# Chunked attention and a squared-ReLU FFN on one core: weight preparation moved from GpSimd to VectorE, the second token tile transposed by TensorE, fewer loads for v

## The chip, the core and the metric

The kernel runs on one core of a Trainium2 chip. The metric is the device time of one execution in microseconds. The engines are named as in the profile: PE (TensorE, the matrix engine; PEld is its weight load), DVE (VectorE), ACT (ScalarE), POOL (GpSimd) and SP (SyncE, which issues all DMAs here). Each engine works off its own instructions strictly in order and waits for others by semaphores.

## The reference: what is computed

Attention inside chunks of 64 tokens, without any link between chunks, followed by a two-layer FFN over all tokens. Shapes: 8 batches, 8 heads, 576 tokens, head dimension 64; the FFN goes 512 -> 2048 -> 512 over 4608 tokens.

```python
scores = scale * np.matmul(q_c, k_c.transpose(0, 1, 2, 4, 3))      # 64x64 per chunk
scores = scores - np.max(scores, axis=-1, keepdims=True)
attn = np.exp(scores)
attn = attn / (np.sum(attn, axis=-1, keepdims=True) + 1e-09)
out = np.matmul(attn, v_c)
x = out.transpose(0, 2, 1, 3).reshape(B * S, H * D)
h = x @ w_in
g = np.where(h >= 1, h, np.where(h <= -1, 0.0, (h + 1) ** 2 / 4))
return (g @ w_out).astype(np.float32)
```

q, k and v are float32; the two weight matrices arrive as float64, 8 bytes an element.

## The kernel before, in words

**Tiles.** The 4608 tokens are nine tiles of 512: tiles 0 to 3 and 5 to 8 are the first 512 tokens of a batch each, tile 4 (`BATCH[4]` is None) collects the last 64 tokens of all eight. In each tile, attention runs in four groups `g` of two heads; the FFN runs in 16 steps `j`, one per block of 128 hidden units.

**Precision.** FFN products use the fast fp32r type with operands split in a high and a low part: `high x high + high x low + low x high`, three matmuls of 512 columns each. `ffn_in` (L528) does twelve per step, `ffn_out` (L563) twelve, two steps behind. `ffn_split` (L548, L549) splits the activation, `attn_split` (L512, L513) the attention output.

**Weight preparation.** There are 32 weight blocks, 16 of `w_in` (wi) and 16 of `w_out` (wo). `load_weight` brings one as raw 64-bit words, 512 KB, into a tile that its two parts later overwrite. `prepare` turns the words into fp32 and splits them. Its steps, in order: ACT copies the upper words' absolute value (L257); DVE raises it to a least value (L260); DVE shifts and masks (L262); DVE merges sign and exponent bits in (L266); ACT scales the lower words to their share of the mantissa (L270); POOL adds the two as integers (L275); ACT rounds to the high part (L282); DVE subtracts for the low part (L286). All preparation happens beside the FFN of the first tile; from then on the weights stay on the chip.

**Attention.** `load_heads` loads q, k and v of a group. `attn_turn` transposes q and k, `scores_of` multiplies, `attn_softmax` normalises (in the first two tiles the last multiply, L477, is on POOL), then the exponentials `e` are transposed to `aT`, `values_of` multiplies by v, and `attn_split` hands on. There are two ways to transpose. In tile 0, PE does it: `flip` (L358) is four 128 x 128 transposes into a PSUM bank, and ACT copies the bank out (L373, L496). From tile 1 on, q and k are loaded block by block (`load_blocks`, L317, four DMAs each) so that a DVE transpose of 32 x 32 blocks finishes the job (L367); `e` is transposed by DVE too (L499) and put in place by eight small DMAs on SP (L489). v is loaded by four DMAs per group (L336).

**What sets the order.** Nothing is reordered by a compiler. `Plan` collects every piece of work with an engine, an estimated cost and what it reads and writes; `Plan.emit` then runs a small list scheduler over these estimates and issues the instructions of each engine in the order in which they would start. `lag` and `moving` are estimates for a DMA's delay and transfer; `port=True` marks pieces that the scheduler keeps from overlapping between DVE and POOL. While PE has nothing to do at the start it is given filler matmuls (L673) until a named PSUM bank is first written. The attention of tile t+1 is planned into the FFN of tile t, one group per four steps; for tile 0, all four groups come first: turn, scores and softmax of each, then values of each. `first_loads` lists the loads of the start in order, with all of v at the end, in front of the first wo block.

Of the kernel before, what the change touches and what calls it, by code (L numbers as in the profile page):

```python
# [9 lines left out]
F32 = mybir.dt.float32  # L10
# [121 lines left out]
def kernel(  # L132
# [15 lines left out]
    nc = tc.nc  # L148
# [46 lines left out]

    o_pair, a_pair = bank_pair("ps_o23"), bank_pair("ps_a")
    o_banks = buffers(psum, "ps_o", 2) + [(f"ps_o{2 + b}", o_pair[:, b, :]) for b in range(2)]
    h_banks = buffers(psum, "ps_h", 2)


# [31 lines left out]
    def load_weight(w, j):  # L232
        def emit():
            words[w, j] = dst = place("words", w, j, [P, 2 * T], U32)
            if w == "wi":
                nc.sync.dma_start(
                    out=dst.rearrange("p (kc f) -> p kc f", kc=KC),
                    in_=w_in[:, 2 * j * P:2 * (j + 1) * P].rearrange(
                        "(kc p) f -> p kc f", p=P
                    ),  # L240
                )
            else:
                nc.sync.dma_start(out=dst, in_=w_out[j * P:(j + 1) * P, :])

        plan.add("sp", 0.6, emit, (), (f"{w}{j}_0", f"{w}{j}_1"), lag=1.7, moving=1.7)

    def prepare(w, j):


        both = (f"{w}{j}_0", f"{w}{j}_1")  # L250
        ykey, yf = turn_of("tmp", tmp_bufs)
        y = yf.bitcast(U32)

        def half(n):
            return words[w, j].rearrange("p (n two) -> p n two", two=2)[:, :, n]

        plan.add("act", 0.52, lambda: nc.scalar.activation(  # L257
            out=yf, in_=half(1).bitcast(F32), func=AF.Abs
        ), both, (ykey,))
        plan.add("dve", 0.34, lambda: nc.vector.tensor_scalar_max(yf, yf, LEAST), (), (ykey,),  # L260
                 port=True)
        plan.add("dve", 0.34, lambda: nc.vector.tensor_scalar(  # L262
            out=y, in0=y, scalar1=3, scalar2=0x3FFFFFFF,
            op0=ALU.logical_shift_left, op1=ALU.bitwise_and,
        ), (), (ykey,), port=True)
        plan.add("dve", 0.6, lambda: nc.vector.scalar_tensor_tensor(  # L266
            out=y, in0=half(1), scalar=0xC0000000, in1=y,
            op0=ALU.bitwise_and, op1=ALU.bitwise_or,
        ), both, (ykey,), port=True)
        plan.add("act", 0.52, lambda: nc.scalar.activation(  # L270
            out=half(0), in_=half(0), func=AF.Copy, scale=2.0 ** -29
        ), (), both)

        def round_up():
            nc.gpsimd.tensor_tensor(out=y, in0=y, in1=half(0), op=ALU.add)  # L275
            words.pop((w, j))

        plan.add("pool", 1.25, round_up, (*both, ykey), (ykey,), port=True)

        def high():  # L280
            weight[w, j] = place("parts", w, j, [P, 2, T], F32R)
            nc.scalar.copy(out=weight[w, j][:, 0, :], in_=yf)  # L282

        def low():
            hi, lo = (weight[w, j][:, n, :] for n in range(2))
            nc.vector.tensor_tensor(out=lo, in0=yf, in1=hi.bitcast(F32), op=ALU.subtract)  # L286
# [40 lines left out]

    def load_values(dst, src, t, g):


        for r in range(2):
            for h in range(2):
                rows = heads_rows(src, t, 2 * g + h)
                into = dst[r * C:(r + 1) * C, h * HALF:(h + 1) * HALF]
                split = "(r n) p d -> r p n d" if t == 0 else "(n r) p d -> r p n d"
                nc.sync.dma_start(  # L336
                    out=into.rearrange("p (n d) -> p n d", d=D),
                    in_=rows.rearrange(split, r=2)[r],
                )

    def load_heads(t, g, which="qkv"):
        for n, src, bufs in (("q", q, q_bufs), ("k", k, k_bufs), ("v", v, v_bufs)):
            if n not in which:
                continue
            key, dst = room(n, bufs, t, g)
            load = load_values if n == "v" else load_rows if t == 0 else load_blocks
            rows, parts = (1.4, 2) if load == load_rows else (1.4, 4) if load == load_values else (
                (2.2, 4) if BATCH[t] is not None else (2.2, 8)
            )
            plan.add(  # L350
                "sp", 0.6 * parts, lambda load=load, dst=dst, src=src: load(dst, src, t, g),
                (), (key,), lag=1.7, moving=rows,
            )

    def flip(ps, src):
# [4 lines left out]
    def attn_turn(t, g):  # L360
        for n, (name, bufs, src_bufs, dst_bufs) in enumerate(
            (("q", "qT", q_bufs, qT_bufs), ("k", "kT", k_bufs, kT_bufs))
        ):
            skey, src = room(name, src_bufs, t, g)
            dkey, dst = room(bufs, dst_bufs, t, g)
            if t > 0:
                plan.add("dve", 0.6, lambda src=src, dst=dst: nc.vector.transpose(  # L367
                    out=dst, in_=src
                ), (skey,), (dkey,))
                continue  # L370
            pkey, ps = o_banks[n]
            plan.add("pe", 0.45, lambda src=src, ps=ps: flip(ps, src), (skey,), (pkey,), columns=T)
            plan.add("act", 0.48, lambda ps=ps, dst=dst: nc.scalar.copy(out=dst, in_=ps),  # L373
                     (pkey,), (dkey,))

    def scores_of(t, g):

        qkey, qT = room("qT", qT_bufs, t, g)  # L380
# [2 lines left out]

        def emit():
            for n in range(CT // 2):
                place = (2 * (n % 2) + n // 2 if t == 0 else n) * C
                for i in range(2):
                    for half in range(2):
                        rows = slice(half * C, (half + 1) * C)
                        at = slice((2 * n + i) * C, (2 * n + i + 1) * C)  # L390
                        nc.tensor.matmul(  # L391
                            out=pair[i * C:(i + 1) * C, half, place:place + C],
                            lhsT=qT[rows, at], rhs=kT[rows, at], start=True, stop=True,
                        )

# [2 lines left out]
    def values_of(t, g):  # L398
# [6 lines left out]
        def emit():  # L405
            for n in range(CT // 2):
                for h in range(2):
                    at = (4 * (n % 2) + 2 * (n // 2) + h) * C if t == 0 else h * HALF + n * C
# [25 lines left out]
    def attn_softmax(t, g):  # L434
# [4 lines left out]
        akey, aT = room("aT", aT_bufs, t, g)  # L439
        e3 = e.rearrange("p (n k) -> p n k", k=C)  # L440
        e4 = e.rearrange("p (h n k) -> p h n k", h=2, k=C)
        mx4 = mx.rearrange("p (h n) x -> p h n x", h=2)
        sc = pair[:, :, :HALF].rearrange("p h (n k) -> p h n k", k=C)

        plan.add("dve", 0.6, lambda: nc.vector.tensor_reduce(  # L445
# [3 lines left out]
        if sums:  # L449
            plan.add("dve", 0.08, lambda: nc.vector.tensor_scalar_mul(mx, mx, -SCALE), (), (mkey,))  # L450

            def exps():
                for n in range(G):
                    nc.scalar.activation(
                        out=e3[:, n, :], in_=sc[:, n // 4, n % 4, :], func=AF.Exp, bias=mx[:, n, :],
                        scale=SCALE, accum_out=sm[:, n, :],
                    )

            plan.add("act", 2.33, exps, (*pkeys, mkey), (ekey, skey))
# [18 lines left out]
            out=e3, in0=e3, in1=sm.broadcast_to([P, G, C]), op=ALU.mult  # L478
        ), (skey,), (ekey,), port=True)

        def move():


# [6 lines left out]
                        out=dst[b:b + Q, :, i // 2, :], in_=src[a:a + Q, :, i % 2, :]  # L490
                    )

        if t == 0:
            pkey, ps = h_banks[0]
            plan.add("pe", 0.45, lambda: flip(ps, e), (ekey,), (pkey,), columns=T)
            plan.add("act", 0.48, lambda: nc.scalar.copy(out=aT, in_=ps), (pkey,), (akey,))  # L496
        else:
# [4 lines left out]
    def attn_split(t, g):  # L502
# [2 lines left out]
        lkey, xl = xl_bufs[g][t % 2]  # L505

        def of_tokens(x):
            split = "p (r n q) -> p r n q" if t == 0 else "p (n r q) -> p r n q"
            return x.rearrange(split, r=2, q=C)
# [63 lines left out]
    def store(t, s):  # L573
# [42 lines left out]

    def load_more(n):
# [15 lines left out]
    for t in range(NTILE + 1):  # L633
        for j in range(NF):
            n = (t + 1) * NP + j // 4
            if (t, j) == (0, 0):
                attn_turn(1, 0)
                attn_products(scores_of(1, 0))
                attn_softmax(1, 0)

            def attention():
                if n >= ALL:
# [4 lines left out]
                if j % 4 == 2:  # L647
                    if n + 1 < ALL:
# [2 lines left out]
                        )  # L651
                        attn_split(*now)
                        attn_softmax(*then)
                    else:
                        attn_products(values_of(*now))
                        attn_split(*now)
# [18 lines left out]
    plan.emit(("pe", 0.215, warm, "ps_h1", 512))  # L675


# [29 lines left out]
```

## Time and profile before

| | us |
|---|---|
| median of 3 runs (lowest to highest) | 904.72 (903.48 to 905.89) |
| profiled execution, device time | 903.74 |
| profiled execution, span | 902.0 |
| PE busy in the span | 870.9 (97%) |
| DVE busy | 468.7 (52%) |
| ACT busy | 382.0 (42%) |
| POOL busy | 59.2 (7%) |

The span is what the instruction records cover; the device time of the same execution is 1.74 us longer. A busy share over the whole span is a mean over unlike stages: the loading and attention of tile 0 (to about 34 us), the FFN of tile 0 with the weight preparation beside it (to about 159 us), and the FFN of tiles 1 to 8. So the rows below are read by stage. In a row of the groups stand the line, engine and operation, what is written and read, shapes and count, then the total busy time and the mean duration of one in ns, then the engine's idle time just before them and what ended it. In a row of the timeline, the first number is the start and the second the duration, both in us.

### The profile page before, as it was taken

How to read it: one execution, taken by the hardware profiler on the slowest of the kernel's cores; microseconds unless marked ns; L12 is line 12 of the kernel's file. 1: busy time of each engine (PE TensorE's matmuls, PEld its weight loads, DVE VectorE, ACT ScalarE, POOL GpSimd, SP SyncE). 2: the span in 40 equal slices, each digit the busy share in tenths (PEclk: the TensorE clock that was granted, in tenths of full speed). 3: DMA queues.
4: the chain of work that ended last, by engine and by line, in shares of the span. 5: the costliest groups of instructions: out<-in, count | busy, mean ns of one | idle time of the engine just before them, and what ended most of it. 6: DMA issues, size and time to landing. Idle time of an engine off the chain costs nothing.

```text
span 902.0 us, 15075 instructions
## 1 busy us (share of the span) xinstructions
PE 870.9 (97%) x5932; PEld 709.6 (79%) x5932; DVE 468.7 (52%) x770; ACT 382.0 (42%) x691; POOL 59.2 (7%) x46
## 2 busy tenths in 40 slices
PE   9888698999999999999999999999999999999998
PEld 8655476788888888888888888888888888888886
DVE  4799889744454445444444444444544454423222
ACT  4687667433343334333433343333333343333332
POOL 1244424100000000000000000000000000000000
PEclk9999988999999999999999999999999999999999
DMA  6788632432232223222322234222322221001001
GB/s 164 222 271 256 152 56 51 104 61 43 49 79 48 47 47 84 51 47 47 88 48 47 45 59 83 48 47 48 94 48 48 47 71 25 12 1 47 0 1 47
DMA packets 268999, 63.93 MB, mean 71 GB/s; under 512 B 254080, under 2 KB 262272, under 8 KB 268928
## 3 DMA queue, kind: packets, MB, share of 16 engines
q1 hardware_dynamic: 268928, 62.96, 31.3%
q8 instruction: 47, 0.77, 0.4%
q14 instruction: 24, 0.20, 0.1%
HBM read 45.09 MB, written 9.44 MB: 60 GB/s over the span
## 4 chain that ended last, share of the span: by engine, by line
PE 84%; DVE 7%; SPq 4%; DMA 2%; ACT 2%; issue 1%; POOL 0%; DVEq 0%; POOLq 0%
PE ps_h L528 40%; PE ps_o L563 40%; PE ps_a L412 2%; PE ps_a L391 2%; SPq L303 1%; DVE tmp L266 1%; SPq L336 1%; DVE tmp L260 1%; DVE tmp L262 1%; SPq L489 1%; DVE gl L549 1%; DVE parts_wi L286 1%; DMA q_sb<-in_q_dram 1%; DMA words_wo<-in_moe_w_out_dram 1%; DVE r L539 1%
## 5 line engine op out<-in xcount | busy, mean ns | idle before, releaser
L528 PE MATMUL ps_h<-xh,parts_wi 128*128 128x512 f32 x1152 | 388.9, 398 | 6.1 <-ACT parts_wi L282 5.0
L563 PE MATMUL ps_o<-parts_wo,gh 128*128 128x512 f32 x1152 | 357.9, 391 | 9.1 <-DVE parts_wo L286 4.6
L528 PEld LDWEIGHTS ps_h<-xh,parts_wi 128*128 128x128 f32 x1152 | 218.0, 190 | 58.5 <-ACT parts_wi L282 6.9
L563 PEld LDWEIGHTS ps_o<-parts_wo,gh 128*128 128x128 f32 x1152 | 216.6, 188 | 59.0 <-DVE parts_wo L286 7.7
L539 DVE SCALAR_TENSOR_TENSOR r<-ps_h,r 128x512 f32<-128x512 f32 x144 | 97.9, 680 | 265.4 <-ACT r L538 265.4
L528 PE MATMUL ps_h<-xl,parts_wi 128*128 128x512 f32 x576 | 226.8, 394 | 0.0
L563 PE MATMUL ps_o<-parts_wo,gl 128*128 128x512 f32 x576 | 224.4, 390 | 0.9 <-DVE gl L549 0.9
L535 ACT ACTIVATE r<-ps_h 128x512 f32<-128x512 f32 x144 | 86.2, 598 | 265.1 <-PE ps_h L528 262.6
L549 DVE TENSOR_TENSOR gl<-r,gh 128x512 fp32r<-128x512 f32 x144 | 101.5, 705 | 107.1 <-ACT gh L548 106.9
L548 ACT CAST gh<-r 128x512 fp32r<-128x512 f32 x144 | 89.6, 622 | 153.6 <-PE ps_o L563 113.3
L563 PEld LDWEIGHTS ps_o<-parts_wo,gl 128*128 128x128 f32 x576 | 108.2, 188 | 23.8 <-DVE gl L549 1.6
L528 PEld LDWEIGHTS ps_h<-xl,parts_wi 128*128 128x128 f32 x576 | 109.4, 190 | 21.8
L538 ACT ACTIVATE r<-r 128x512 f32<-128x512 f32 x144 | 90.9, 631 | 3.5
L512 ACT CAST xh<-ps_a 128x512 fp32r<-128x512 f32 x34 | 20.0, 588 | 48.2 <-DVE mx L445 39.4
L412 PEld LDWEIGHTS ps_a<-aT,v_sb 64*64 64x64 f32 x1056 | 19.4, 136 | 16.7 <-issue 16.6
L470 DVE TENSOR_REDUCE sm<-e 128x8 f32<-128x512 f32 x30 | 20.6, 686 | 19.4 <-ACT e L464 18.6
L445 DVE TENSOR_REDUCE mx<-ps_a 128x8 f32<-128x512 f32 x34 | 23.3, 686 | 13.5 <-PE ps_a L391 9.8
L412 PE MATMUL ps_a<-aT,v_sb 64*64 64x64 f32 x1056 | 24.2, 227 | 5.1 <-DMA aT<-x 5.1
L275 POOL TENSOR_TENSOR tmp<-tmp,words_wo 128x512 uint32<-128x512 uint32 x16 | 26.2, 1635 | 38.3 <-ACT words_wo L270 19.9
L275 POOL TENSOR_TENSOR tmp<-tmp,words_wi 128x512 uint32<-128x512 uint32 x16 | 23.2, 1451 | 39.2 <-ACT words_wi L270 33.2
L513 DVE TENSOR_TENSOR xl<-ps_a,xh 128x512 fp32r<-128x512 f32 x34 | 23.5, 691 | 3.2 <-ACT xh L512 2.2
L499 DVE STREAM_TRANSPOSE x<-e 128x512 f32<-128x512 f32 x32 | 22.7, 709 | 0.9
(73 smaller groups left out, 437.9 us busy)
## 6 DMA issues: line engine op xcount, KB each, us to landing
v_sb<-in_v_dram SPq DMA_DIRECT2D x136, 64.0 KB, 2.5
words_wi<-in_moe_w_in_dram SPq DMA_DIRECT2D x16, 512.0 KB, 7.1
words_wo<-in_moe_w_out_dram SPq DMA_DIRECT2D x16, 512.0 KB, 7.6
aT<-x SPq DMA_DIRECT2D x256, 32.0 KB, 1.9
out_dram<-tmp SPq DMA_DIRECT2D x32, 256.0 KB, 2.0
q_sb<-in_q_dram SPq DMA_DIRECT2D x112, 64.0 KB, 2.3
k_sb<-in_k_dram SPq DMA_DIRECT2D x112, 64.0 KB, 2.3
q_sb<-in_q_dram SPq DMA_DIRECT2D x32, 32.0 KB, 2.1
```

Source lines behind the costliest of these rows:

```text
L275: nc.gpsimd.tensor_tensor(out=y, in0=y, in1=half(0), op=ALU.add)
L412: nc.tensor.matmul(out=pair[h * C:(h + 1) * C, half, HALF + n * C:HALF + (n + 1) * C], lhsT=v_sb[rows, of:of + C], rhs=aT[rows, at:at + C] ...
L445: plan.add("dve", 0.6, lambda: nc.vector.tensor_reduce(out=mx4, in_=sc, axis=AX.X, op=ALU.max), pkeys, (mkey,))
L499: plan.add("dve", 0.6, lambda: nc.vector.transpose(out=x, in_=e), (ekey,), (xkey,))
L513: plan.add("dve", 0.6, lambda: nc.vector.tensor_tensor(out=of_tokens(xl), in0=ps, in1=of_tokens(xh.bitcast(F32)), op=ALU.subtract), (*pkey ...
L528: nc.tensor.matmul(out=ps, lhsT=weight["wi", j][:, half, kc * P:(kc + 1) * P], rhs=x, start=(kc == 0 and i == 0), stop=(kc == KC - 1 and i ...
L535: plan.add("act", 0.48, lambda: nc.scalar.activation(out=r, in_=ps, func=AF.Relu, bias=0.5, scale=0.5), (pkey,), (rkey,))
L538: plan.add("act", 0.52, lambda: nc.scalar.square(out=r, in_=r), (), (rkey,))
L539: plan.add("dve", 0.6, lambda: nc.vector.scalar_tensor_tensor(out=r, in0=ps, scalar=1.0, in1=r, op0=ALU.max, op1=ALU.min), (pkey,), (rkey,))
L548: plan.add("act", 0.52, lambda: nc.scalar.copy(out=gh, in_=r), (rkey,), (ghkey,))
L549: plan.add("dve", 0.6, lambda: nc.vector.tensor_tensor(out=gl, in0=r, in1=gh.bitcast(F32), op=ALU.subtract), (rkey, ghkey), (glkey,), port ...
L563: nc.tensor.matmul(out=acc, lhsT=x[:, cols], rhs=weight["wo", j][:, half, :], start=(j == 0 and i == 0), stop=(j == NF - 1 and i == 2),)
```

## The change

Four edits. First, `prepare`: the absolute value and the least value go; ACT instead scales the upper words by 2^-112, which brings the exponent down, DVE shifts by three, DVE (not POOL) adds the lower words' share, and DVE merges the sign bit last. Second, the first tile's groups are planned one by one: group g's turn, scores and softmax, then the turn back, values and split of group g-1; the first loads are put in another order. Third, v of a whole-batch tile is loaded by two DMAs per group instead of four. Fourth, `FLIPPED = 2`: tile 1 loads and transposes as tile 0 does, with PE flips through the PSUM banks `a_banks` and ACT copies in place of DVE transposes and the DMAs of `move`. Some estimates of the planner change with this.

```diff
     def prepare(w, j):
...
         plan.add("act", 0.52, lambda: nc.scalar.activation(
-            out=yf, in_=half(1).bitcast(F32), func=AF.Abs
+            out=yf, in_=half(1).bitcast(F32), func=AF.Copy, scale=2.0 ** -112
         ), both, (ykey,))
-        plan.add("dve", 0.34, lambda: nc.vector.tensor_scalar_max(yf, yf, LEAST), (), (ykey,),
-                 port=True)
         plan.add("dve", 0.34, lambda: nc.vector.tensor_scalar(
-            out=y, in0=y, scalar1=3, scalar2=0x3FFFFFFF,
-            op0=ALU.logical_shift_left, op1=ALU.bitwise_and,
+            out=y, in0=y, scalar1=3, scalar2=None, op0=ALU.logical_shift_left
         ), (), (ykey,), port=True)
-        plan.add("dve", 0.6, lambda: nc.vector.scalar_tensor_tensor(
-            out=y, in0=half(1), scalar=0xC0000000, in1=y,
-            op0=ALU.bitwise_and, op1=ALU.bitwise_or,
-        ), both, (ykey,), port=True)
         plan.add("act", 0.52, lambda: nc.scalar.activation(
             out=half(0), in_=half(0), func=AF.Copy, scale=2.0 ** -29
         ), (), both)
-        def round_up():
-            nc.gpsimd.tensor_tensor(out=y, in0=y, in1=half(0), op=ALU.add)
+        plan.add("dve", 0.6, lambda: nc.vector.tensor_tensor(
+            out=y, in0=y, in1=half(0), op=ALU.add
+        ), both, (ykey,), port=True)
+
+        def sign():
+            nc.vector.scalar_tensor_tensor(
+                out=y, in0=half(1), scalar=0x80000000, in1=y,
+                op0=ALU.bitwise_and, op1=ALU.bitwise_or,
+            )
             words.pop((w, j))
-        plan.add("pool", 1.25, round_up, (*both, ykey), (ykey,), port=True)
+        plan.add("dve", 0.6, sign, both, (ykey,), port=True)
...
     def load_values(dst, src, t, g):
-        for r in range(2):
-            for h in range(2):
-                rows = heads_rows(src, t, 2 * g + h)
-                into = dst[r * C:(r + 1) * C, h * HALF:(h + 1) * HALF]
-                split = "(r n) p d -> r p n d" if t == 0 else "(n r) p d -> r p n d"
+        for h in range(2):
+            rows = heads_rows(src, t, 2 * g + h)
+            into = dst[:, h * HALF:(h + 1) * HALF].rearrange("p (n d) -> p n d", d=D)
+            if BATCH[t] is not None:
+                nc.sync.dma_start(out=into, in_=rows.rearrange("(n r) p d -> (r p) n d", r=2))
+                continue
...
-            load = load_values if n == "v" else load_rows if t == 0 else load_blocks
+            load = load_values if n == "v" else load_rows if t < FLIPPED else load_blocks
...
-            if t > 0:
+            if t >= FLIPPED:
                 plan.add("dve", 0.6, lambda src=src, dst=dst: nc.vector.transpose(
                     out=dst, in_=src
                 ), (skey,), (dkey,))
                 continue
-            pkey, ps = o_banks[n]
+            pkey, ps = o_banks[n] if t == 0 else a_banks[n]
...
-        if t == 0:
-            pkey, ps = h_banks[0]
+        if t < FLIPPED:
+            pkey, ps = h_banks[1] if t == 0 else a_banks[0]
             plan.add("pe", 0.45, lambda: flip(ps, e), (ekey,), (pkey,), columns=T)
             plan.add("act", 0.48, lambda: nc.scalar.copy(out=aT, in_=ps), (pkey,), (akey,))
...
     first_loads = [
-        ("q", 0), ("k", 0), ("q", 1), ("k", 1), ("q", 2), ("k", 2), ("wi", 0), ("q", 3), ("k", 3),
-        ("wi", 1), ("v", 0), ("v", 1), ("v", 2), ("v", 3),
+        ("q", 0), ("k", 0), ("q", 1), ("k", 1), ("wi", 0), ("q", 2), ("k", 2), ("v", 0), ("q", 3),
+        ("k", 3), ("v", 1), ("wi", 1), ("v", 2), ("v", 3),
     ]
...
-    for g in range(NP):
-        attn_turn(0, g)
-        attn_products(scores_of(0, g))
-        attn_softmax(0, g)
-    for g in range(NP):
-        attn_products(values_of(0, g))
-        attn_split(0, g)
+    for g in range(NP + 1):
+        if g < NP:
+            attn_turn(0, g)
+            attn_products(scores_of(0, g))
+            attn_softmax(0, g)
+        if g > 0:
+            attn_turn_back(0, g - 1)
+            attn_products(values_of(0, g - 1))
+            attn_split(0, g - 1)
...
     def warm():
-        nc.tensor.matmul(out=h_banks[1][1][:, :P], lhsT=ident, rhs=ident, start=True, stop=True)
+        nc.tensor.matmul(out=h_banks[0][1][:, :P], lhsT=ident, rhs=ident, start=True, stop=True)
```

`attn_turn_back` is the end of the former `attn_softmax` (transposing `e`), made a function of its own; `flip` is unchanged.

More of the change, by code (lines that the diff above doesn't have):

```diff
@@ L166 @@
     ALL = NTILE * NP
+    FLIPPED = 2
     BATCH = (0, 1, 2, 3, None, 4, 5, 6, 7)
@@ L197 @@
     o_banks = buffers(psum, "ps_o", 2) + [(f"ps_o{2 + b}", o_pair[:, b, :]) for b in range(2)]
+    a_banks = [(f"ps_a{b}", a_pair[:, b, :]) for b in range(2)]
     h_banks = buffers(psum, "ps_h", 2)
@@ L243, in emit @@
                 nc.sync.dma_start(out=dst, in_=w_out[j * P:(j + 1) * P, :])
-        plan.add("sp", 0.6, emit, (), (f"{w}{j}_0", f"{w}{j}_1"), lag=1.7, moving=1.7)
+        plan.add("sp", 0.57, emit, (), (f"{w}{j}_0", f"{w}{j}_1"), lag=2.1, moving=1.9)
     def prepare(w, j):
@@ L328, in load_values @@
     def load_values(dst, src, t, g):
-        for r in range(2):
-            for h in range(2):
-                rows = heads_rows(src, t, 2 * g + h)
-                into = dst[r * C:(r + 1) * C, h * HALF:(h + 1) * HALF]
-                split = "(r n) p d -> r p n d" if t == 0 else "(n r) p d -> r p n d"
+        for h in range(2):
[4 more added lines that the diff above has]
+                continue
+            for r in range(2):
                 nc.sync.dma_start(
-                    out=into.rearrange("p (n d) -> p n d", d=D),
-                    in_=rows.rearrange(split, r=2)[r],
+                    out=into[r * C:(r + 1) * C],
+                    in_=rows.rearrange("(n r) p d -> r p n d", r=2)[r],
                 )
@@ L345, in load_heads @@
             key, dst = room(n, bufs, t, g)
-            load = load_values if n == "v" else load_rows if t == 0 else load_blocks
-            rows, parts = (1.4, 2) if load == load_rows else (1.4, 4) if load == load_values else (
-                (2.2, 4) if BATCH[t] is not None else (2.2, 8)
-            )
+            load = load_values if n == "v" else load_rows if t < FLIPPED else load_blocks
+            parts = 4 if load == load_blocks else 2
+            if BATCH[t] is None:
+                parts *= 2
             plan.add(
-                "sp", 0.6 * parts, lambda load=load, dst=dst, src=src: load(dst, src, t, g),
-                (), (key,), lag=1.7, moving=rows,
+                "sp", 0.67 * parts, lambda load=load, dst=dst, src=src: load(dst, src, t, g),
+                (), (key,), lag=2.1, moving=2.2 if load == load_blocks else 1.35,
             )
@@ L385, in emit @@
             for n in range(CT // 2):
-                place = (2 * (n % 2) + n // 2 if t == 0 else n) * C
                 for i in range(2):
@@ L391, in emit @@
                         nc.tensor.matmul(
-                            out=pair[i * C:(i + 1) * C, half, place:place + C],
+                            out=pair[i * C:(i + 1) * C, half, n * C:(n + 1) * C],
                             lhsT=qT[rows, at], rhs=kT[rows, at], start=True, stop=True,
@@ L438, in attn_softmax @@
         ekey, e = room("e", e_bufs, t, g)
-        akey, aT = room("aT", aT_bufs, t, g)
         e3 = e.rearrange("p (n k) -> p n k", k=C)
-        e4 = e.rearrange("p (h n k) -> p h n k", h=2, k=C)
+        e4 = e.rearrange("p (n h k) -> p h n k" if t < FLIPPED else "p (h n k) -> p h n k", h=2, k=C)
         mx4 = mx.rearrange("p (h n) x -> p h n x", h=2)
+        sm4 = sm.rearrange("p (n h) x -> p h n x" if t < FLIPPED else "p (h n) x -> p h n x", h=2)
         sc = pair[:, :, :HALF].rearrange("p h (n k) -> p h n k", k=C)
@@ L454, in exps @@
                     nc.scalar.activation(
-                        out=e3[:, n, :], in_=sc[:, n // 4, n % 4, :], func=AF.Exp, bias=mx[:, n, :],
-                        scale=SCALE, accum_out=sm[:, n, :],
+                        out=e4[:, n // 4, n % 4, :], in_=sc[:, n // 4, n % 4, :], func=AF.Exp,
+                        bias=mx[:, n, :], scale=SCALE, accum_out=sm4[:, n // 4, n % 4, :],
                     )
@@ L479, in attn_softmax, with attn_turn_back @@
         ), (skey,), (ekey,), port=True)
+    def attn_turn_back(t, g):
+        ekey, e = room("e", e_bufs, t, g)
+        akey, aT = room("aT", aT_bufs, t, g)
         def move():
@@ L639 @@
                 attn_softmax(1, 0)
+                attn_turn_back(1, 0)
             def attention():
@@ L653, in attention @@
                         attn_softmax(*then)
+                        attn_turn_back(*then)
                     else:
@@ L672, in warm @@
     def warm():
-        nc.tensor.matmul(out=h_banks[1][1][:, :P], lhsT=ident, rhs=ident, start=True, stop=True)
-    plan.emit(("pe", 0.215, warm, "ps_h1", 512))
+        nc.tensor.matmul(out=h_banks[0][1][:, :P], lhsT=ident, rhs=ident, start=True, stop=True)
+    plan.emit(("pe", 0.215, warm, "ps_h0", 512))
 _INS = ['q', 'k', 'v', 'moe_w_in', 'moe_w_out']
```

6 lines of the change are left out of this document (2 added, 4 removed).

## The prediction

> **What bounds the kernel now.** I read the busy time by stretches first, to find where TensorE is not full.
>
> ```profile
> 14.00:166.00 152.00, 126.51 (x968) 95.94 (x968) 135.49 (x222) 105.46 (x230) 58.00 (x40) 0.94 0.59 159
> 34.00:159.00 125.00, 103.91 (x653) 76.40 (x652) 113.66 (x185) 90.65 (x205) 51.11 (x34) 0.93 0.61 165
> 159.00:898.00 739.00, 738.57 (x4857) 606.70 (x4855) 336.35 (x554) 275.01 (x461) 1.64 (x1) 1.00 0.25 50
> ```
>
> Columns are PE, PEld, DVE, ACT, POOL busy, then the granted clock, the DMA share and GB/s. From 159 us on PE is busy 738.57 of 739 us at full clock: nothing that spares another engine shortens that part. From 34 to 159 us, DVE is the fullest engine (113.66 of 125, 91%). This is the FFN of the first token tile, with the 32 weight blocks being prepared beside it.
>
> How much PE work lies in that stretch? The timeline gives its two ends, the first FFN matmul of tile one and of tile two:
>
> ```profile
> 33.70 0.50 PE L528 MATMUL ps_h<-xh,parts_wi 128*128 128x512 f32 x1
> 158.84 0.39 PE L528 MATMUL ps_h<-xh,parts_wi 128*128 128x512 f32 x1
> ```
>
> The chain of waits gives the price of 12 matmuls at full clock, and the length of a tile:
>
> ```profile
> 171.48 2.95 PE ps_h L528 x12
> 174.43 2.72 PE ps_o L563 x12
> 263.80 2.95 PE ps_h L528 x12
> ```
>
> One tile takes 263.80 - 171.48 = 92.32 us; 32 x 2.72 = 87.04 of it are FFN products, so one attention group costs (92.32 - 87.04)/4 = 1.32. The groups of PE between 33 and 158.8 us:
>
> ```profile
> L528 PE MATMUL ps_h<-xh,parts_wi 128*128 128x512 f32 x128 | 49.4, 444 | 6.1 <-ACT parts_wi L282 5.0 <-DVE parts_wi L286 0.9
> L563 PE MATMUL ps_o<-parts_wo,gh 128*128 128x512 f32 x112 | 37.8, 408 | 9.1 <-DVE parts_wo L286 4.6 <-ACT parts_wo L282 4.4
> L412 PE MATMUL ps_a<-aT,v_sb 64*64 64x64 f32 x128 | 4.0, 246 | 5.1 <-DMA aT<-x 5.1
> ```
>
> With one low-part matmul to two high ones, that is 192 + 168 = 360 matmuls, 30 x 2.72 = 81.6 us, and four attention groups and a half, 5.9: together 87.5 us of work in 158.84 - 33.70 = 125.1 us. The other 37.6 us is the most that can be won behind 33.7 us. PE's idle time there ends on weight parts from ACT L282 and DVE L286, and on the move of aT by DMA.
>
> **Why DVE is full.** Its groups from 14 to 166 us, and the GpSimd add beside them:
>
> ```profile
> L262 DVE TENSOR_SCALAR tmp<-tmp 128x512 uint32<-128x512 uint32 x32 | 22.9, 730 | 0.0
> L260 DVE TENSOR_SCALAR tmp<-tmp 128x512 f32<-128x512 f32 x32 | 19.8, 641 | 2.6 <-ACT tmp L257 2.5
> L549 DVE TENSOR_TENSOR gl<-r,gh 128x512 fp32r<-128x512 f32 x16 | 14.1, 884 | 0.0
> L286 DVE TENSOR_TENSOR parts_wi<-tmp,parts_wi 128x512 fp32r<-128x512 f32 x16 | 12.0, 749 | 1.3 <-ACT parts_wi L282 1.2
> L266 DVE SCALAR_TENSOR_TENSOR tmp<-words_wi,tmp 128x512 uint32<-128x512 uint32 x16 | 11.9, 741 | 0.1
> L266 DVE SCALAR_TENSOR_TENSOR tmp<-words_wo,tmp 128x512 uint32<-128x512 uint32 x16 | 11.7, 734 | 0.0
> L286 DVE TENSOR_TENSOR parts_wo<-tmp,parts_wo 128x512 fp32r<-128x512 f32 x16 | 11.2, 699 | 1.9 <-ACT parts_wo L282 1.9
> L367 DVE STREAM_TRANSPOSE qT<-q_sb 128x512 f32<-128x512 f32 x6 | 4.2, 700 | 0.0
> ...
> L275 POOL TENSOR_TENSOR tmp<-tmp,words_wo 128x512 uint32<-128x512 uint32 x16 | 26.2, 1635 | 38.3 <-ACT words_wo L270 19.9 <-DVE tmp L266 7.2 <-DMA v_sb<-in_v_dram 3.5
> L275 POOL TENSOR_TENSOR tmp<-tmp,words_wi 128x512 uint32<-128x512 uint32 x16 | 23.2, 1451 | 39.2 <-ACT words_wi L270 33.2 <-DVE tmp L260 3.0 <-DVE tmp L266 1.6
> ```
>
> On the timeline, one GpSimd add:
>
> ```profile
> 62.74 1.36 POOL L275 TENSOR_TENSOR tmp<-tmp,words_wo 128x512 uint32<-128x512 uint32 x1 [3.75 <-DVE tmp L266]
> ```
>
> DVE in the same moments:
>
> ```profile
> 62.86 1.79 DVE L549 TENSOR_TENSOR gl<-r,gh 128x512 fp32r<-128x512 f32 x1
> 64.57 0.41 DVE L262 TENSOR_SCALAR tmp<-tmp 128x512 uint32<-128x512 uint32 x1
> 64.91 0.41 DVE L260 TENSOR_SCALAR tmp<-tmp 128x512 f32<-128x512 f32 x1
> 65.24 0.68 DVE L266 SCALAR_TENSOR_TENSOR tmp<-words_wi,tmp 128x512 uint32<-128x512 uint32 x1
> 65.85 0.68 DVE L286 TENSOR_TENSOR parts_wo<-tmp,parts_wo 128x512 fp32r<-128x512 f32 x1
> ```
>
> Undisturbed, a shift lasts 0.41 us and a two-input operation 0.68; back to back they start 0.34 and 0.60 apart. Beside the GpSimd add, L549 lasts 1.79 and ends just after the add does. The excess of the group means over the undisturbed durations is time in which DVE stands behind GpSimd: 32 x (0.730 - 0.41) = 10.2, 32 x (0.641 - 0.41) = 7.4, 16 x (0.884 - 0.68) = 3.3, L286 23.2 - 32 x 0.68 = 1.4, L266 23.6 - 21.8 = 1.8: 24.1 us in all.
>
> **The change, part by part.**
>
> *The add leaves GpSimd.* Of GpSimd's 58.00 us in this stretch the adds are 26.2 + 23.2 = 49.4; the softmax multiplies of the first two tiles (the other 8.6) stay. So about 49.4/58.00 = 85% of the excess goes: -20.5. The DVE pass of L260 goes and a two-input add comes; shift, sign merge and low part stay. No row shows an integer add on DVE; the nearest, L266 (integers, one strided input) and L286 (a subtract), both start 0.60 apart. Below, 0.34 if it ran like a shift; above, the 1.36 of the GpSimd add. I take 0.60: 32 x (0.60 - 0.34) = +8.3. At 1.36 it would be +32.6 and the whole gain on DVE would be gone; at 0.34 it would be zero. ACT has the same three passes. The add now waits on DVE itself for ACT's scaling (L270), where GpSimd idled 53 us for it; queued behind it would be the FFN's L539 and L549 and then PE. But L270 no longer has to follow L266, which reads the same words, so it can run straight behind L257. I price this wait inside the utilisation below.
>
> *The second tile is flipped by TensorE.* DVE loses q, k and e transposes of four groups: 12 x 0.60 = -7.2 at the spacing of other full-width operations (-8.4 by the 0.70 of L367's row). PE gains 12 flips; the timeline has two of them in a row:
>
> ```profile
> 18.59 0.60 PE L358 MATMUL ps_o<-ident,first_wi 128*128 128x128 f32 x4
> 19.03 0.60 PE L358 MATMUL ps_h<-ident,e 128*128 128x128 f32 x4
> ```
>
> ACT gains 12 evacuations; one of them, with what stood around it when tile one's last group came in:
>
> ```profile
> 26.89 1.72 SPq L243 DMA_DIRECT2D words_wo<-in_moe_w_out_dram  x1
> ...
> 31.89 0.66 ACT L257 ACTIVATE tmp<-words_wo 128x512 f32<-128x512 f32 x1 [3.30 <-DMA words_wo<-in_moe_w_out_dram]
> 32.45 0.57 ACT L496 COPY first_wi<-ps_h 128x512 f32<-128x512 f32 x1
> 33.07 0.69 PE L412 MATMUL ps_o<-first_wi,first_wo 64*64 64x64 f32 x32 [2.57 <-ACT first_wi L496]
> ```
>
> Two flips follow 0.44 apart: 12 x 0.44 = +5.3 on PE. A copy is 0.57: 12 x 0.53, between that and a tighter spacing, is +6.4 on ACT. On SP 32 DMAs of aT, half of the q and k issues and half of the v issues of tile two go, and with them PE's 5.1 us of waits for aT. SP is not the bound in this stretch; I give that no term of its own.
>
> *Sum for the stretch.* Scaled to the 29 preparations of the stretch, DVE's net of -20.5 + 8.3 - 7.2 = -19.4 becomes -17.6 to -19 (the excess is denser in it, as 51.11 of the 58.00 us of GpSimd lie there), so 113.7 falls to 94.7 to 96.1. ACT rises from 90.65 to 97 by durations, which shrink to some 91 when it runs back to back. PE needs 87.5 + 5.3 = 92.8. Three engines then stand within 4% of each other, where one was the bound. Before, the bound engine was 91% busy. With three interlocked I choose 88%, an estimate, on the lower value: 94.7/0.88 = 107.6 in place of 125.1, a gain of 17.5. At 91% it would be 21.0, at 84% 12.4, and with PE never waiting (92.8) 32.3.
>
> *The first tile group by group, and v in half as many DMAs.* The FFN's start waited for the fourth group's values; their input copy (ACT L496, 32.45) stood behind ACT L257, which waited 3.30 us for the first w_out block, issued at 26.89 behind sixteen v DMAs. Eight fewer at this spacing:
>
> ```profile
> 15.90 5.21 SPq L336 DMA_DIRECT2D v_sb<-in_v_dram  x8
> ```
>
> 5.21/8 = 0.65 each, 5.2 us off that issue. So the 3.3 us wait goes: FFN start 33.7 to about 30.4. Bounds: +1.3 if only the later issue of the fourth group's q and k (two v DMAs ahead) is felt, -5.2 if all that SP saves arrives. I take -3.3. The other edits (the layout of e in tile one, which h bank the warm-up writes) change no instruction count: nothing, as they lie under loads.
>
> Total -17.5 - 3.3 = -20.8. The profiled execution took 903.74 us (span 902.0 and 1.74 around it), 1.0 below the median of 904.72, within the spread of the runs: 903.74 - 20.8 = 882.9, so **883**.
>
> **The rivals.**
>
> 1. *Three engines wait in turn* (ACT hands to DVE, DVE to ACT, both to PE), and utilisation falls to 80%: 94.7/0.80 = 118.4, a gain of 6.7 + 3.3, so 894. For it: PE's own waits end on both ACT L282 and DVE L286. Against: the preparation's chain gets shorter, one engine fewer.
> 2. *PE becomes the bound and stays full.* 92.8 + about 3 of first waits: gain 29 + 3.3, so 871. Against: ACT and DVE have no room either.
> 3. *The new PE-ACT-PE round trips stall PE: slower.* A flip goes through PSUM and ACT, and what is queued in order behind the scores and values on PE waits. PE waited 2.57 us for one such copy at 33.07. Were all 12 flips to cost that, 12 x 2.57 = 31 on top: 883 + 31 = 914; from 1.75 us each (20.8/12) the change loses. Against: a group has some 25 us, and other PE work is placed between.
> 4. *The clock drops around the flips: slower.* In these rows PE ran at little over half clock for 8 us after a wait, which costs 8 x 0.43 = 3.4 us:
>
> ```profile
> 112.00:116.00 4.00, 2.51 (x64) 0.58 0.07 12
> 116.00:120.00 4.00, 4.00 (x12) 0.56 0.35 77
> ```
>
> Two such drops in each of four groups would be 27.5 us: 910. Against: the first tile's flips ran at 1.00, though among warm-up matmuls, and later flips are short beside FFN products.
> The Trainium skill, "TensorE: Matmul & The Clock Gate", Part 4 (PE-mode transpose), says that a transpose does not count as PE-busy for the gate; by that rule this rival would be the likely one wherever flips stand alone. No run here shows flips without other matmuls around them.
> 5. *No change*: the weights' arrival sets the pace, 903. Against: the idle times for weight DMAs in the DVE and ACT rows are single ones of about 3 us.
>
> **How the numbers follow.** Forecast 0.63, own range 876 to 889 (84% to 92%); rival 1 0.17, rival 2 0.11, rival 3 0.04, rival 4 0.03, rival 5 0.02. The range 871 to 896 takes in rivals 1 and 2 and leaves out the tails. Faster by over 0.3% (2.7 us, about what this kernel's runs can tell) is 0.63 + 0.17 + 0.11 and a little, less what an add near 1.36 would take: 0.92; within it 0.03, slower 0.05.
>
> **What would show it.** In the changed profile: DVE shifts near 0.41 in the mean and L549's counterpart near 0.68 in this stretch; the add at 0.60 to 0.68; first FFN matmul at about 30; PE full from about 138, where it was 159; the steady 92.3 us a tile untouched. Wrong if the add lasts over 1 us, if the fullest engine stays below 80%, or if PE's idle time ends on the flips' copies or comes with a clock under 0.9.

## The result, and the profile after

| | us | ratio to before, 95% interval |
|---|---|---|
| before (median of 4 runs) | 904.74 | |
| changed kernel (median of 4 runs, 877.76 to 878.51) | **877.93** | 0.9705 [0.9688, 0.9722] |
| predicted | 883 (871 to 896) | |

The change makes the kernel 26.8 us (3%) faster. The span of the changed kernel is 876.2 us, 25.8 less than before. Here is where it ends up, by the stretches of the changed kernel (columns as in the prediction: PE, PEld, DVE, ACT, POOL busy, clock, DMA share, GB/s):

```profile
33.70:133.60 99.90, 95.76 (x711) 77.00 (x704) 95.96 (x176) 88.92 (x212) 4.76 (x4) 0.97 0.62 173
116.00:872.00 756.00, 756.00 (x4993) 621.38 (x4991) 344.99 (x575) 284.10 (x476) 0.00 (x0) 1.00 0.25 49
```

The end part is as full as before, so what was won lies ahead of it. The timeline of PE gives the first FFN matmul of the first tile, the first one of the second, and the value products (L413) of two attention groups in a row, one on either side of it:

```profile
20.52 0.48 PE L532 MATMUL ps_h<-xh,parts_wi 128*128 128x512 f32 x1
...
121.51 0.69 PE L413 MATMUL ps_a<-aT,v_sb 64*64 64x64 f32 x32
...
133.62 0.39 PE L532 MATMUL ps_h<-xh,parts_wi 128*128 128x512 f32 x1
...
144.59 0.69 PE L413 MATMUL ps_a<-aT,v_sb 64*64 64x64 f32 x32
```

The second tile's FFN starts at 133.62 where it was 158.84: 25.2 of the 25.8 us. Four times 144.59 - 121.51 is 92.3, the same steady tile. DVE is now 96% busy from 33.7 us to the second tile (95.96 of 99.9); it was 113.66 of 125 us. This is not quite the same stretch of work: the first tile's FFN used to start at 33.70 us and now starts at 20.52. DVE's groups from 14 to 150 us:

```profile
L262 DVE TENSOR_SCALAR tmp<-tmp 128x512 uint32<-128x512 uint32 x32 | 14.1, 462 | 0.0
L553 DVE TENSOR_TENSOR gl<-r,gh 128x512 fp32r<-128x512 f32 x18 | 12.8, 712 | 2.8 <-ACT gh L552 2.5
L288 DVE TENSOR_TENSOR parts_wo<-tmp,parts_wo 128x512 fp32r<-128x512 f32 x16 | 12.4, 772 | 0.2 <-ACT parts_wo L284 0.2
...
L269 DVE CUSTOM_DVE_ANT_0 tmp<-words_wo,tmp 128x1024 uint16<-128x1024 uint16 x16 | 11.5, 716 | 0.4 <-ACT words_wo L265 0.4
L269 DVE CUSTOM_DVE_ANT_0 tmp<-words_wi,tmp 128x1024 uint16<-128x1024 uint16 x16 | 11.2, 698 | 0.0
```

The shift fell from a mean of 0.730 to 0.462 us, the activation's low part (L549, now L553) from 0.884 to 0.712. The add, L269, takes 0.71 in the mean. PE's own waits for other work, from 17 us on:

```profile
PE ps_a L361 <- POOL e L478: 2.6, 2, 2.5
PE ps_o L392 <- DVE xl L517: 2.1, 1, 2.1
PE ps_h L532 <- ACT xh L516: 1.7, 1, 1.7
PE ps_o L413 <- ACT first_wi L501: 1.2, 1, 1.2
```

The waits for weight parts and for aT are gone. In the kernel before, the same view from 30 to 165 us has 19.1 us of them in its first four rows:

```profile
PE ps_a L412 <- DMA aT<-x: 5.1, 3, 2.7
PE ps_h L528 <- ACT parts_wi L282: 5.0, 3, 3.2
PE ps_o L563 <- DVE parts_wo L286: 4.6, 5, 2.0
PE ps_o L563 <- ACT parts_wo L282: 4.4, 4, 1.9
```

In the changed kernel PE waits after 52 us, in the whole rest of the run, for this much:

```profile
PE ps_a L361 <- ACT qT L376: 0.7, 1, 0.7
PE ps_a L361 <- POOL e L478: 0.2, 1, 0.2
```

### The profile page after: what moved, and what is told of

It is laid out like the page before. It is cut to its first block, busy times and chain, and to the rows that moved or that the text cites. A ratio compares the mean times of both kernels' runs of the same rounds, so it can differ in the third digit from the quotient of the medians.

```text
span 876.2 us, 14898 instructions
## 1 busy us (share of the span) xinstructions
PE 860.7 (98%) x5942; PEld 707.5 (81%) x5942; DVE 445.0 (51%) x758; ACT 382.4 (44%) x703; POOL 9.9 (1%) x14
## 4 chain that ended last, share of the span: by engine, by line
PE 90%; DVE 3%; DMA 1%; ACT 1%; SPq 1%; issue 1%; POOL 0%; POOLq 0%; DVEq 0%; ACTq 0%
PE ps_o L567 43%; PE ps_h L532 43%; PE ps_a L413 2%; PE ps_a L392 1%; DMA words_wo<-in_moe_w_out_dram 1%; DVE tmp L269 1%; SPq L244 1%; PE ps_a L361 1%; DVE tmp L274 0%; DMA k_sb<-in_k_dram 0%; SPq L319 0%; POOL e L478 0%; ACT tmp L259 0%; DVE mx L446 0%; DVE tmp L262 0%
## 5 line engine op out<-in xcount | busy, mean ns | idle before, releaser
L532 PE MATMUL ps_h<-xh,parts_wi 128*128 128x512 f32 x1152 | 384.9, 394 | 2.1 <-ACT xh L516 1.7
L553 DVE TENSOR_TENSOR gl<-r,gh 128x512 fp32r<-128x512 f32 x144 | 98.8, 686 | 109.7 <-ACT gh L552 109.4
L413 PEld LDWEIGHTS ps_a<-aT,v_sb 64*64 64x64 f32 x1056 | 18.4, 134 | 11.4 <-issue 10.9
L413 PE MATMUL ps_a<-aT,v_sb 64*64 64x64 f32 x1056 | 22.9, 224 | 0.0
L392 PE MATMUL ps_a<-kT,qT 64*64 64x64 f32 x1056 | 21.4, 218 | 0.4 <-ACT kT L376 0.4
L504 DVE STREAM_TRANSPOSE x<-e 128x512 f32<-128x512 f32 x28 | 19.9, 711 | 0.9
L370 DVE STREAM_TRANSPOSE qT<-q_sb 128x512 f32<-128x512 f32 x28 | 19.7, 702 | 0.0
```

The costliest lines, as they stand in the source:

```text
L392: nc.tensor.matmul(out=pair[i * C:(i + 1) * C, half, n * C:(n + 1) * C], lhsT=qT[rows, at], rhs=kT[rows, at], start=True, stop=True,)
L413: nc.tensor.matmul(out=pair[h * C:(h + 1) * C, half, HALF + n * C:HALF + (n + 1) * C], lhsT=v_sb[rows, of:of + C], rhs=aT[rows, at:at + C] ...
L532: nc.tensor.matmul(out=ps, lhsT=weight["wi", j][:, half, kc * P:(kc + 1) * P], rhs=x, start=(kc == 0 and i == 0), stop=(kc == KC - 1 and i ...
L553: plan.add("dve", 0.6, lambda: nc.vector.tensor_tensor(out=gl, in0=r, in1=gh.bitcast(F32), op=ALU.subtract), (rkey, ghkey), (glkey,), port ...
```

## The experiments

The first kernel is the kernel before with one part of the change; each of the others is the changed kernel with one edit, or with the two or three that its name says. Times are medians; a difference is taken between ratios to the kernel before on the same chip, as that kernel itself came to 903.2 to 904.7 us in the several comparisons. (Some expectations below count from raw medians of different chips: 5.8 and 3.7 us there are 4.4 and 2.5 here.)

| kernel | us | ratio, 95% interval | against the change, us |
|---|---|---|---|
| before + new preparation alone | 886.43 | 0.9809 [0.9781, 0.9837] | |
| old preparation back | 893.12 | 0.9885 [0.9861, 0.9910] | +16.3 |
| second tile by DVE | 882.95 | 0.9778 [0.9756, 0.9799] | +6.6 |
| v in four DMAs | 878.09 | 0.9719 [0.9698, 0.9740] | none shown |
| old loads and groups | 872.08 | 0.9656 [0.9638, 0.9674] | -4.4 |
| old groups alone | 872.22 | 0.9659 [0.9644, 0.9675] | -4.2 |
| spare GpSimd work | 893.29 | 0.9887 [0.9865, 0.9909] | +16.5 |
| all multiplies on DVE | 878.32 | 0.9720 [0.9702, 0.9738] | none shown |
| h banks exchanged | 874.26 | 0.9677 [0.9658, 0.9695] | -2.5 |
| old start and exchanged banks | 872.80 | 0.9669 [0.9649, 0.9689] | -3.3 |
| old start, k by ACT's queue | 874.09 | 0.9679 [0.9661, 0.9697] | -2.4 |
| warm-up by transposes | 876.88 | one run | none shown |

### The preparation: alone, and taken back

Alone, the function `prepare` of the changed kernel stands in the kernel before; taken back, it is the other way round.

```diff
-        plan.add("pool", 1.25, round_up, (*both, ykey), (ykey,), port=True)
+        plan.add("dve", 0.6, lambda: nc.vector.tensor_tensor(
+            out=y, in0=y, in1=half(0), op=ALU.add
+        ), both, (ykey,), port=True)
```

> The kernel before with the new weight preparation and nothing else. Theory A (the GpSimd adds held DVE up and DVE set the pace): of DVE's 113.7 us in the stretch about 19 go and 7.5 come, 102 remain; at 92% to 96% busy that is 107 to 111 in place of 125.1, so a gain of 14 to 18 us: 886 to 890. Theory B (the gain comes from the start and from SP being freed of DMAs): under 5 us, 899 or more.

> The changed kernel with the old preparation on GpSimd put back, all else as changed. Theory A: DVE's load in the stretch rises by about 19 - 7.5 = 11.5 us and sets the pace again: 877.9 + 11 to 13, 889 to 891. Theory B: at most 4 us lost, 882.

Alone it brings 16.8 us (903.19 to 886.43; the interval allows 14.7 to 19.8), taken back it costs 16.3, more than the 11 to 13 expected. Both fit theory A in kind and rule out B as the main cause. With the old preparation back, the old rows return: a long low part beside a GpSimd add, and PE waits for weight parts (groups from 14 to 150 us, and PE's waits from 34 to 160 us).

```profile
L554 DVE TENSOR_TENSOR gl<-r,gh 128x512 fp32r<-128x512 f32 x15 | 17.6, 1177 | 0.7 <-ACT gh L553 0.5
...
L278 POOL TENSOR_TENSOR tmp<-tmp,words_wo 128x512 uint32<-128x512 uint32 x16 | 26.3, 1644 | 33.4 <-ACT words_wo L273 20.7 <-DVE tmp L269 12.7
```

```profile
PE ps_o L568 <- DVE parts_wo L289: 4.4, 5, 1.4
```

### Contention or chain? Spare work on GpSimd

Taking the GpSimd step away shortens the chain of a preparation and also ends the contention. Spare work, for which nobody waits, brings back only the contention.

```diff
         plan.add("dve", 0.6, low, (ykey, both[0]), (both[1],), port=True)
+
+        def spare():
+            hi, lo = (weight[w, j][:, n, :].bitcast(U32) for n in range(2))
+            for n in range(2):
+                cols = slice(n * HALF, (n + 1) * HALF)
+                nc.gpsimd.tensor_tensor(out=scratch, in0=hi[:, cols], in1=lo[:, cols], op=ALU.add)
+
+        plan.add("pool", 1.25, spare, both, ("scratch",))
```

> The changed kernel plus spare work on GpSimd: after each low part, two integer adds of 128x256 over that weight block into a scratch tile that nobody reads. Nothing waits for them, so the chain of a preparation stays as short as in the changed kernel. Theory A (DVE stands behind GpSimd's operations): DVE's means rise to the level of before (shift 0.7 in place of 0.46 us), about 20 us more on DVE, which is 96% busy: 893 to 898. Rival C (the loss before was the GpSimd step inside the chain, not the contention): 878.

It costs 16.5 us, as theory A has it. The groups of DVE and POOL:

```profile
L263 DVE TENSOR_SCALAR tmp<-tmp 128x512 uint32<-128x512 uint32 x32 | 21.9, 704 | 0.0
L270 DVE CUSTOM_DVE_ANT_0 tmp<-words_wo,tmp 128x1024 uint16<-128x1024 uint16 x16 | 15.0, 940 | 0.0
...
L562 DVE TENSOR_TENSOR gl<-r,gh 128x512 fp32r<-128x512 f32 x15 | 13.3, 889 | 0.0
...
L298 POOL TENSOR_TENSOR scratch<-parts_wo 128x256 uint32<-128x256 uint32 x32 | 39.1, 1222 | 28.1 <-DVE parts_wo L289 26.4
```

Shift 0.704 and low part 0.889 are the figures of before (0.730 and 0.884). In its stretch DVE is 99.7% busy:

```profile
33.70:150.00 116.30, 105.06 (x720) 83.54 (x713) 115.97 (x176) 91.48 (x211) 70.62 (x64) 0.90 0.55 153
```

Part of the loss is another one: PE waited 8.1 us for multiplies of the softmax that stood behind spare work on GpSimd, 2.6 in the changed kernel.

```profile
PE ps_a L370 <- POOL e L487: 8.1, 4, 2.8
```

Nor is the dose quite the old one: the spare adds have as many elements as the old ones (64 of 256 columns for 32 of 512), but they take 69.7 us of GpSimd, not 49.4, and they lack the mark `port=True` by which the planner kept the old adds away from DVE. So the experiment shows that work on GpSimd for which nobody waits is enough to bring DVE's long means back and to lose time of this size. It does not show that every one of the 16.5 us is contention (some 5.5 may be the longer waits for the multiplies), and how much of the gain of the change is due to the shorter chain stays open.

### What is left of GpSimd

```diff
-        on_pool = t < 2
+        on_pool = False
```

> The changed kernel with the softmax multiply of the first two tiles on DVE too, so that GpSimd does nothing but make the identity. It adds 8 x 0.60 = 4.8 us to DVE, takes away what is left of the excess (shift mean 0.46 against 0.41 undisturbed, low part 0.77 against 0.68: about 5 us) and PE's wait of 2.6 us for the multiply. If the remaining contention and that wait weigh: 875 to 877. If DVE's own load weighs: 880.

Neither number came: no change in time can be told. The rows are clean now, the shift at its undisturbed mean, and DVE carries the eight multiplies for it:

```profile
L262 DVE TENSOR_SCALAR tmp<-tmp 128x512 uint32<-128x512 uint32 x32 | 12.7, 418 | 0.0
```

### The second tile's transposes

```diff
-    FLIPPED = 2
+    FLIPPED = 1
```

> The changed kernel with the second tile transposed by DVE and moved by DMA as before (FLIPPED = 1), all else as changed. If DVE (and the waits for aT) still matter: 12 transposes of 0.6 us back on DVE, 5 to 8 us lost, 883 to 886. Rival: PE, which is full from 48 us on in the changed kernel, is the only bound, and the 12 flips of 0.44 us were a loss: 873.

q and k of that tile are loaded block by block again, too. The kernel loses 6.6 us, so the flips are a gain though PE is full. Without them PE waits again, from 34 to 160 us:

```profile
PE ps_o L567 <- DVE parts_wo L288: 2.7, 5, 1.1
PE ps_a L413 <- DMA aT<-x: 2.3, 1, 2.3
```

### v in four DMAs

```diff
         for h in range(2):
             rows = heads_rows(src, t, 2 * g + h)
             into = dst[:, h * HALF:(h + 1) * HALF].rearrange("p (n d) -> p n d", d=D)
-            if BATCH[t] is not None:
-                nc.sync.dma_start(out=into, in_=rows.rearrange("(n r) p d -> (r p) n d", r=2))
-                continue
             for r in range(2):
```

> The changed kernel with v in four DMAs per group again (half the partitions each), all else as changed. By the prediction: eight more issues of about 0.65 us ahead of the first w_out block, 5.2 us later there; between 1 and 5 us lost, 879 to 883. Rival: SP has slack because PE waits for attention and DVE in the first 48 us: 878.

The first w_out block is issued at 25.23 us in this kernel (first row) and at 19.80 in the changed one (second row), 5.4 us apart, and the time is the same. The prediction's count of SP was right and is worth nothing here, with the first tile planned group by group; with the old groups it was not tried.

```profile
25.23 0.60 SPq L244 DMA_DIRECT2D words_wo<-in_moe_w_out_dram  x1
```

```profile
19.80 1.14 SPq L244 DMA_DIRECT2D words_wo<-in_moe_w_out_dram  x1
```

### The start

First the whole old start (order of loads and of groups), then the old groups alone:

```diff
-    for g in range(NP + 1):
-        if g < NP:
-            attn_turn(0, g)
-            attn_products(scores_of(0, g))
-            attn_softmax(0, g)
-        if g > 0:
-            attn_turn_back(0, g - 1)
-            attn_products(values_of(0, g - 1))
-            attn_split(0, g - 1)
+    for g in range(NP):
+        attn_turn(0, g)
+        attn_products(scores_of(0, g))
+        attn_softmax(0, g)
+        attn_turn_back(0, g)
+    for g in range(NP):
+        attn_products(values_of(0, g))
+        attn_split(0, g)
```

> The changed kernel with the old order of the first loads and of the first tile's groups (all scores, then all values). By the prediction's term for the start: about 2 to 4 us lost, 880 to 882 (v still in two DMAs). Theory B: 8 us or more lost, 886. If the first tile's order only shuffles work that PE does later anyway: 878.

> The changed kernel with only the first tile's groups planned as before (all scores, then all values) and the new order of the first loads kept. If the 5.8 us between the changed kernel and the one with the whole old start come from planning the groups one by one (FFN products of step 0 go out early at 20.5 us, the warm-up ends with them, and PE then waits at 0.5 of the clock): 872 to 874. If they come from the order of the loads: 877 to 878.

None of the numbers expected of the first was right: the old start is faster, by 4.4 us, and nearly all of it comes with the old groups. PE in stretches of 4 us (busy, clock, DMA share, GB/s), first the changed kernel, then the one with the old groups:

```profile
20.00:24.00 4.00, 2.09 (x43) 1.00 0.88 245
24.00:28.00 4.00, 2.65 (x71) 1.00 1.08 387
28.00:32.00 4.00, 2.57 (x7) 0.68 1.18 299
32.00:36.00 4.00, 2.85 (x41) 0.50 1.11 356
36.00:40.00 4.00, 3.62 (x45) 0.97 1.06 409
```

```profile
20.00:24.00 4.00, 3.85 (x81) 1.00 1.06 286
24.00:28.00 4.00, 3.03 (x73) 1.00 0.98 346
28.00:32.00 4.00, 3.57 (x48) 1.00 0.92 136
32.00:36.00 4.00, 3.03 (x17) 1.00 0.94 304
36.00:40.00 4.00, 3.29 (x43) 1.00 1.08 386
```

Warm-up matmuls stop for good when the first FFN product writes its bank (`ps_h0`). With the groups one by one that is at 20.52 us, in the middle of the attention; PE then waits for groups three and four with nothing to fill the time, and its clock falls to half. With the old groups the first FFN product comes at 23.80 us and PE finds more to do behind it. Exchanging the h banks lets the warm-up go on until FFN step 1, with the order of the groups as changed:

```diff
-            pkey, ps = h_banks[1] if t == 0 else a_banks[0]
+            pkey, ps = h_banks[0] if t == 0 else a_banks[0]
...
-        nc.tensor.matmul(out=h_banks[0][1][:, :P], lhsT=ident, rhs=ident, start=True, stop=True)
+        nc.tensor.matmul(out=h_banks[1][1][:, :P], lhsT=ident, rhs=ident, start=True, stop=True)
...
-    plan.emit(("pe", 0.215, warm, "ps_h0", 512))
+    plan.emit(("pe", 0.215, warm, "ps_h1", 512))
```

> The changed kernel with the two h banks of the first tile exchanged as they were before: e is flipped through the first, warm-up matmuls write the second, so they go on until FFN step 1. In the changed kernel the clock granted between 28 and 36 us is 0.5 to 0.7, which costs some 2.7 us of full-rate PE time. If that weighs: 875 to 876. If the first FFN products now wait for the flips in the same bank: 878 to 880.

> The whole old start together with the exchanged h banks (warm-up until FFN step 1). If the two gains of 5.8 and 3.7 us are the same thing, a warm-up that lasts until FFN work is there, they don't add: 871 to 873. If they are two things: 868 to 869.

The exchange alone wins 2.5 us of the 4.4 (its interval overlaps that of the changed kernel by a little; on its own chip, "v in four DMAs" and "all multiplies on DVE", which changed nothing, took 878.1 and 878.3 us for its 874.3). On top of the old start it wins nothing. So the two are at least in great part one thing: PE kept busy until there is FFN work. The exchange moves more than the fillers, though: step 0 now shares its bank with the flips of e, and in the trace the first FFN product comes at 27.77 us in place of 20.52, right behind the last fillers. Whether the clock or the later, closer start of the FFN wins the time was not taken apart, nor what makes the remaining 2 us.

> The whole old start, with k of the first tile issued from ACT's queue, so that SP issues eight DMAs less in the first 14 us. If SP's issue time (0.65 us each) sets when the groups arrive: the first FFN products come 2 to 4 us earlier, 868 to 870. If the transfers themselves do (DMA share 0.77 in the first 16 us, 1.0 behind it), or ACT's own queue is held up by issuing: 872 or more.

```diff
+        queue = nc.scalar if t == 0 and src is k else nc.sync
         for j in range(2):
-            nc.sync.dma_start(
+            queue.dma_start(
...
-                "sp", 0.67 * parts, lambda load=load, dst=dst, src=src: load(dst, src, t, g),
+                "act" if t == 0 and n == "k" else "sp", 0.67 * parts, lambda load=load, dst=dst, src=src: load(dst, src, t, g),
```

This is no faster than the old start without it (0.9679 against 0.9656, intervals overlap), so taking issues off SP did not bring the start forward. The first FFN product comes later, not earlier, at 28.23 us (first row) against 25.52 with the old start (second row); whether the transfers or ACT's queue hold it was not taken apart.

```profile
28.23 0.50 PE L533 MATMUL ps_h<-xh,parts_wi 128*128 128x512 f32 x1
```

```profile
25.52 0.50 PE L532 MATMUL ps_h<-xh,parts_wi 128*128 128x512 f32 x1
```

### Do transposes keep the clock up?

```diff
-        nc.tensor.matmul(out=h_banks[0][1][:, :P], lhsT=ident, rhs=ident, start=True, stop=True)
+        nc.tensor.transpose(out=h_banks[0][1][:, :P], in_=ident, identity=ident)
```

> The changed kernel with its warm-up matmuls replaced by 128x128 PE transposes of the same size, so that PE runs almost nothing but transposes in the first 20 us. By the rule that rival 4 rests on (a transpose does not count as busy for the clock gate), the granted clock from 0 to 20 us is about 0.5, where the changed kernel has 1.00, and the time rises to 880 or more. If a transpose counts like a matmul: 1.00 there, 878.

They do. PE's timeline and its stretches:

```profile
1.36 2.82 PE L681 MATMUL ps_h<-ident 128*128 128x128 f32 x12 [1.36 <-POOL ident masks.py:199]
4.55 1.06 PE L361 MATMUL ps_o<-ident,q_sb 128*128 128x128 f32 x4 [0.36 <-DMA q_sb<-in_q_dram]
5.43 0.62 PE L681 MATMUL ps_h<-ident 128*128 128x128 f32 x4
```

```profile
8.00:12.00 4.00, 3.04 (x51) 1.00 1.09 277
12.00:16.00 4.00, 3.27 (x55) 1.00 1.12 224
16.00:20.00 4.00, 3.10 (x52) 1.00 1.00 256
```

The first four of q take 1.06 us, the next four fillers 0.62: PE got up to speed by 5.4 us having run nothing but transposes. In the changed kernel, with matmuls as fillers, it did so at about the same time (four in the half microsecond to 5.50 us, six in the next). By the groups of PE up to 20 us, transposes make 14.3 of the 18.4 us of all matmuls, and the granted clock stayed at 1.00 to 28 us. The Trainium skill, "TensorE: Matmul & The Clock Gate", Part 4 (PE-mode transpose), states that a transpose does not count as PE-busy; for these fp32 transposes the trace differs, and the measurement decides. The stretch from 0 to 4 us is given as 1.00 too, though its matmuls ran at the slow spacing, so the clock row is not to be trusted before the first change of clock.

## Why the prediction was right, and where its steps were not

**What bounds the kernel, and the GpSimd term: right.** DVE's operations stood beside GpSimd's and lasted longer for it, and the new preparation is the largest part: 16 to 17 us by both experiments. Like is compared with like over the whole run: DVE's busy time fell from 468.7 to 445.0 us, 23.7 where 19.4 were forecast. The preparation alone takes 13.0 off (forecast 20.5 - 8.3 = 12.2), and the flips 9.1 (445.0 against 454.1 without them; forecast 7.2). Spare GpSimd work brings the means of the rows back.

**The add at 0.60: right.** That was a spacing, and on the timeline one add starts 0.60 us ahead of the operation behind it (31.83 and 32.43). Its duration is 0.71 in the mean; the bound of 1.36 played no part. On DVE it waited for ACT's scaling 0.4 us in all.

**The flips: right in kind.** The prediction gave no separate price; taken back, they are worth 6.6 us. Rival 3, stalls on the new round trips through ACT, is refuted: PE's waits on the copies of q and k and on the multiply ahead of e sum to 3.7 us, against the 20.8 that would have been needed. Rival 4, a clock that drops around each group's flips, did not come either: from 52 us on the clock is 1.00. Only around the second tile's first group did it drop: its q and k are flipped at about 34 us, in the drop of the start (0.68 and 0.50 from 28 to 36 us, rows above), and its e at 46.16, behind PE's wait of 2.5 us for the multiply:

```profile
44.00:48.00 4.00, 1.84 (x7) 0.81 0.76 206
48.00:52.00 4.00, 4.00 (x15) 0.76 1.06 383
```

So the prediction's own sign of being wrong, idle time of PE with a clock under 0.9, did show. Both drops follow waits of PE; the transposes above show that PE can come up to full speed on transposes alone.

**Utilisation at 88%: wrong, the mis-sized term.** The step said that three interlocked engines would keep each other waiting more than one bound engine had, and divided DVE's load by 88%. From the first FFN matmul to the second tile DVE was 95% busy (first row; 91% before), and from 48 us on PE, DVE and ACT were 99%, 96% and 88% busy at once (second row):

```profile
20.52:133.62 113.10, 103.13 (x836) 82.10 (x835) 107.86 (x198) 99.29 (x231) 6.85 (x6) 0.95 0.67 190
48.00:133.60 85.60, 84.66 (x617) 68.44 (x616) 82.12 (x151) 75.59 (x176) 3.38 (x3) 0.99 0.55 150
```

In the later part rival 2 (PE stays full) is what happened; after 52 us PE waited 0.9 us in all (0.7 and 0.2, the last two rows on the result). The stretch was to win 17.5 us; preparation (16.3 to 16.8) and flips (6.6) together won about 23, some 5.5 more. A likely reason, argued and not shown: the order is fixed by estimates, and operations that last 0.4 or 1.5 us depending on GpSimd can't be planned, while undisturbed ones meet their estimates. (By the prediction's own sum 84% and 92% give 888 and 878; its range of 876 to 889 is a little wider than that.)

**The start at -3.3: about right in its sum, by luck, and wrong in its parts.** Between "before + new preparation alone" and "second tile by DVE" lie the edits of the start, the layout of e, v in two DMAs and the planner's estimates. The ratios are 0.9809 and 0.9778: 2.8 us won, with intervals that overlap. But the FFN did not start at 30.4 us as forecast: it started at 20.52, because the groups came one by one, and that planning costs 4.2 us. With the old groups the FFN starts at 23.80 or 25.52 us, earlier than the forecast's far bound allowed (33.7 - 5.2), and the kernel is faster still; so what else belongs to the start must be worth some 7 us there (2.8 + 4.2, an estimate that takes the parts to add up). Which of it, the v loads (they issue the first w_out block at 19.51 us in the old start, 26.89 before) or the estimates, no run takes apart. That the bank which the warm-up writes changes nothing failed as well: in the new order of groups this choice moves 2.5 us.

So the 883 for 878 is in the main one error, a stretch booked about 5.5 us too low. The start's -3.3 held only because a loss that was not foreseen stands against a gain that was larger than foreseen.

The version with the old groups and all else as changed, 872.2 us, beats both kernels (0.9659 [0.9644, 0.9675]).

## What to carry to other kernels

When a group's mean is well above the duration of the same operation on a quiet stretch, look for what runs on GpSimd at that moment: the price of a GpSimd operation is then the time for which others stand behind it, and not its own busy time off the path. Taking 49 us of adds away was worth 16 us here. Engines with loads close to each other can still be nearly full together, here at 99%, 96% and 88%. When parts are measured one by one, compare the same work and not the same window: a start that moves shifts the window's contents. And when work at the start is reordered, ask what ends the warm-up: a first product that comes early and alone can cost more than it brings.

## What was not expected of the hardware

The integer add of 512 words ran on DVE as a custom operation over 1024 16-bit elements, at 0.68 us in the median of its row (0.71 in the mean), no longer than a plain two-input operation of 512 elements. And PE came up to speed on transposes alone.
